# Routing attention and a PReLU FFN on one core: one more pair of heads in cluster order

## The chip, the cores and the metric

The kernel runs on one core of a Trainium2 chip. The metric is device microseconds of one execution. TensorE is PE here (PEld its weight loads), VectorE is DVE, ScalarE is ACT, GpSimd is POOL and SyncE, which issues most transfers, is SP. All engines run their own queue in order.

## The reference

```python
# q, k, v: (4, 8, 768, 64); centroids: (8, 16, 64); w_in: (512, 2048); w_out: (2048, 512)
q_assign = argmax(einsum(q_n, c_n)); k_assign = argmax(einsum(k_n, c_n))   # 16 clusters
mask = q_assign[:, :, :, None] == k_assign[:, :, None, :]
scores = where(mask, q @ k.T / sqrt(64), -1e9)
attn = softmax(scores)
x = (attn @ v).transpose(0, 2, 1, 3).reshape(4 * 768, 512)
h = x @ w_in
out = (maximum(h, 0) + alpha * minimum(h, 0)) @ w_out
```

A query attends only to the keys of its own cluster. The weights come as 64-bit floats and all arithmetic is in 32-bit floats.

## The kernel before, in words

**Pairs and forms.** Two heads make a pair (one in each half of the 128 partitions); pair n is heads 2(n % 4) and 2(n % 4) + 1 of batch n // 4, so there are 16 pairs. Pairs 0 to 8 are dense: for each half of the queries (384) and each of six chunks of 128 keys, PE makes the scores (`score`, L784), ACT the exponential, DVE masks other clusters out (`mask`, L825; in batch 0 PE does that, L793), PE weighs the values (`weigh`, L939), DVE sums the denominators (`add_up`, `turn`, `rows_sums`) and multiplies by the inverse (`normalise`, L1042). Pairs 9 to 15 (`n >= NO`) are ordered: tokens are first sorted by cluster, so that a chunk of keys meets only a window of 224, 320 or 384 of the 768 queries (`window`, `weigh_near` L972, `normalise_near`).

**Ordering a pair.** `load` fetches q and k; `order_features` transposes them (L567); `order_sims` makes the similarities (PE, L575); `order_counts`, `order_begins`, `order_ranks` and `order_rows` turn them into a destination row for each token (DVE, with two tiny products L601). Then `order_stage` loads q, k and v rows into a stage tile (three SP transfers, L661) and `order_scatter` writes each 128 rows to a DRAM scratch by an indirect DMA from POOL (L675): six stages of four scatters. `pace` puts a token from ACT ahead of the scatters of a slot (L651, L652), so that POOL doesn't run ahead. `order_load` reads the sorted pair back (L688 to L706), `order_blocks` transposes it (L713). After the attention the rows go back to token order: `to_rows` (PE transposes L1002), twelve scatters `put_back` (POOL, L1011), `fetch_back` and `turn_back` (L1030).

**Steps and slots.** The program is one hand-written order. `steps` lists the attention steps, three for a half of a dense pair or for a whole ordered pair; a step has five slots (`tick`), and `later` files a piece for a later slot. `load_at` and `prep_at` hold the loads and preparations by step (`ORDERS`: where an ordered pair is loaded; `LEADS`: how many steps before its own start it is read back). FFN pieces of the previous half batch (`ffn_pieces`: `hidden` L1066 with the slope L1058, `final` L1084) are fed evenly between, so that PE always has work. Steps 0 to 23 are batch 0. There, `second_part` has not yet been called: raw buffers, conversion tiles and the members of batch 0 lie in the memory that later holds sorting tiles and five more E tiles.

**Conversion of the weights.** In batch 0, 32 blocks of 128x512 weights come as 64-bit words into one of five raw buffers (`fetch`, L247). `split` (DVE) takes them apart, `scale` (ACT) runs four slots later, `join` (DVE and a product on POOL, L271) two slots after that; the `power` tile between them has three buffers. A raw buffer is free after the join.

**Order of batch 1.** Steps 24 to 47: pairs 4, 5, 6, 7, first halves then second halves, each block of twelve steps with the FFN of one half batch.

Of the kernel before, what the change touches and what calls it, by code (L numbers as in the profile page):

```python
# [23 lines left out]
def kernel(  # L24
# [50 lines left out]
    ps_f = fast.enter_context(tc.tile_pool(name="ps_f", bufs=2, space=PS))  # L75
    fast.enter_context(tc.manual_schedule())
    first_part = fast.enter_context(ExitStack())
    memp = first_part.enter_context(tc.tile_pool(name="memp", bufs=NCH))
    raws = first_part.enter_context(tc.tile_pool(name="raws", bufs=1))
    cvt = first_part.enter_context(tc.tile_pool(name="cvt", bufs=3))  # L80

# [22 lines left out]
    pairs = [(b, hp) for b in range(B) for hp in range(NCH)]  # L104
    NO = WHOLE * NCH - 3
    NP = len(pairs)
# [134 lines left out]

    raw_tiles = [raws.tile([P, CW, 2], U32, name=f"raw{i}") for i in range(5)]

    def convert(src, dst):
        raw = raw_tiles[0]
        raw_tiles.append(raw_tiles.pop(0))
        nc.sync.dma_start(out=raw.rearrange("p n w -> p (n w)"), in_=src)  # L247
        lo, hi = raw[:, :, 0], raw[:, :, 1]
        power = []

        def split():
            power.append(cvt.tile([P, CW], U32, name="power"))
            nc.vector.tensor_scalar(out=power[0], in0=hi, scalar1=0x7FF00000, scalar2=None,
                                    op0=ALU.bitwise_and)
            nc.vector.tensor_scalar(out=dst.bitcast(U32), in0=hi, scalar1=0x000FFFFF,
                                    scalar2=None, op0=ALU.bitwise_and)

        def scale():
            nc.scalar.activation(out=power[0], in_=power[0], func=AF.Relu,
                                 bias=low_exp[:, 0:1], scale=8.0)  # L260
            nc.scalar.activation(out=dst, in_=dst.bitcast(U32), func=AF.Identity,
                                 bias=1.0, scale=2.0 ** -20)

        def join():
            nc.vector.scalar_tensor_tensor(
                out=power[0], in0=hi, scalar=0x80000000, in1=power[0],
                op0=ALU.bitwise_and, op1=ALU.bitwise_or)
            nc.vector.scalar_tensor_tensor(  # L268
                out=dst, in0=lo, scalar=2.0 ** -52, in1=dst,
                op0=ALU.mult, op1=ALU.add)  # L270
            nc.gpsimd.tensor_tensor(out=dst, in0=dst, in1=power[0].bitcast(FP32),  # L271
                                    op=ALU.mult)
        return [split, scale, join]
# [23 lines left out]
    def advance(stages):  # L297
        stages.pop(0)()
        if stages:
            later(4 if len(stages) == 2 else 2, lambda: stages and advance(stages))  # L300
        elif stages is under_way[0]:
            under_way.popleft()
            converted[0] += 1
# [186 lines left out]
    STAGES = 2  # L490
    us, ranks, orders, scratch, sorts = {}, {}, {}, {}, {}
    sorting = deque()

    def second_part():

        first_part.close()
        for name, bufs in (("emore", 1), ("ordc", 1), ("ordp", 1), ("order", NP - NO),
                           ("xmore", 1), ("byrow", 1), ("pace", 8)):
            sorts[name] = fast.enter_context(tc.tile_pool(name=name, bufs=bufs))
        for i in range(5):  # L500
            e_tiles.insert(0, sorts["emore"].tile([P, 2, HS], FP32, name=f"more{i}"))

    def order_constants():

        ordc = sorts["ordc"]
        stage = [ordc.tile([P, NX // PARTS, P], FP32, name=f"stage{i}") for i in range(STAGES)]
        place = ordc.tile([P, HS], U16, name="place")
# [8 lines left out]
        brief = asg.tile([P, HS], FP32, name="simT")  # L516
        assert NX // PARTS > len(kinds)
        own = stage[0][:, 0:len(kinds), :]
        for i, pattern in enumerate(kinds):
# [10 lines left out]
        def columns():  # L530
            nc.vector.tensor_reduce(out=cols, in_=own, axis=AX.X, op=ALU.add)
            for t in stage:
                nc.gpsimd.memset(t, 0.0)

# [24 lines left out]
        for i, piece in enumerate((columns, sums_before, sums_within, shifts)):  # L559
            later(5 + i, piece)  # L560
        begins = ordc.tile([P, NP - NO], FP32, name="begins")
        sorts.update(stage=stage, number=number, place=place, before=before, within=within,
                     shift=shift, begins=begins)
# [41 lines left out]
    def order_ranks(n, ps):  # L605
# [3 lines left out]
        nc.vector.tensor_tensor(out=begin, in0=ps[:, 0:2], in1=sorts["shift"], op=ALU.add)  # L609
        nc.vector.tensor_copy(out=sorts["begins"][:, n - NO:n - NO + 1], in_=ps[:, 0:1])  # L610
        nc.vector.scalar_tensor_tensor(out=count, in0=count, scalar=begin[:, 1:2],
# [3 lines left out]
    def order_rows(n, begin, count):  # L615
# [9 lines left out]
        whole = tc.dram_tile([2 * 2 * S, P], FP32, name=f"scratch{n}")  # L625
        scratch[n] = whole, dram_disjoint_views(whole, 2 * NX)
        for i in range(2 * PARTS + STAGES):
            if i >= STAGES:
                for x in range(NX // PARTS):
                    sorting.append((1, lambda i=i - STAGES, x=x: order_scatter(n, i, x)))  # L630
            if i < 2 * PARTS:
                sorting.append((0, lambda i=i: order_stage(n, i)))
        later(2, lambda: order_clusters(n, begin))
# [20 lines left out]
    def order_stage(n, i):  # L654

        b, hp = pairs[n]
        h, part = divmod(i, PARTS)
# [71 lines left out]
    for b in range(B):  # L729
        whole = [n for n in range(b * NCH, (b + 1) * NCH) if n >= NO]  # L730
        rest = [n for n in range(b * NCH, (b + 1) * NCH) if n < NO]
        begun_at.append(len(steps))
        steps += [(n, None, s) for n in whole for s in range(SB)]
        for half in range(2) if rest else ():
            if half and not whole:
                begun_at.append(len(steps))
            steps += [(n, half, s) for n in rest for s in range(SB)]
            feeds[len(steps)] = [(b, 0), (b, 1)] if whole else [(b, half)]
    begun_at.append(len(steps))
# [137 lines left out]
    def rows_sums(n, half):  # L877
        near = n >= NO
        if not near or half == 0:
# [31 lines left out]
    def spread_out(n, half, inv):  # L911
        pool = sorts["ordp"] if n >= NO and half else rdp
        rd = rds[n, half] = pool.tile([P, HS], FP32, name="rd")
# [120 lines left out]
    def x_tile(b, half):  # L1034
        if (b, half) not in xTs:
            pool = sorts["xmore"] if (b, half) == (WHOLE - 1, 1) else xpool
            xTs[b, half] = pool.tile([P, NCH, HS], FP32, name="xT")
# [104 lines left out]
    def last_pieces():  # L1142
# [197 lines left out]
        def room_for_y():  # L1340
            t = sorts["xmore"].tile([P, NCH, HS], FP32, name="xT").rearrange(
                "p c q -> p (c q)")
# [24 lines left out]

    ORDERS = [26, 29, 35, 38, 41, 56, 60]
    LEADS = [4, 3, 4, 4, 3, 3, 3]
    prep_at, load_at = {}, {}  # L1370
    for (n, half), u in start_of.items():
        def at(step, slot, piece):
            prep_at.setdefault((step, slot), []).append(piece)
        if half is None:
            t = ORDERS[n - NO]
            load_at.setdefault(t, []).append(lambda n=n: load(n))
            for i in range(2):
                at(t + 1, FIRST + i, lambda n=n, i=i: order_features(n, i))
            at(t + 2, 2, lambda n=n: order_sims(n))
            load_at.setdefault(u - LEADS[n - NO], []).append(  # L1380
                lambda n=n: order_load(n))
            at(u - 4, 0, lambda n=n: prep_clusters(n))
            for i in range(2):
                at(u - 1, i, lambda n=n, i=i: order_blocks(n, i))
                at(u - 1, FIRST + i, lambda n=n, i=i: order_queries(n, i))
            continue
        if half == 0:
# [5 lines left out]
            else:  # L1393
                load_at.setdefault(u - (9 if u < 2 * TOGETHER else 10), []).append(
                    lambda n=n: load(n))
# [4 lines left out]
            else:  # L1400
                for w in range(2):
                    at(u - 7, FIRST + w + (u - 7 == TOGETHER - 1),
                       lambda n=n, w=w: prep_blocks(n, w))
            at(u - (3 if n < NCH else 5 if u - 6 < TOGETHER else 6), FIRST,
               lambda n=n: prep_sims(n)) if u - 6 < 2 * TOGETHER else at(
                   u - 6, FIRST + 1, lambda n=n: prep_sims(n))
# [14 lines left out]
    def scatters_at(v, s, i):  # L1421


        if v < SB:
            return 1 + (s == 0 or i == 0)
        if v < 3 * SB:
            return 0
        if v < 4 * SB:
            return int(s == 0 or i == 0)
        return 1 + (s == 0 or i % 2 == 0)  # L1430

# [29 lines left out]
    for u in range(-AHEAD, TOGETHER):  # L1461
        for piece in load_at.get(u, []):
            piece()
        n, half, s = steps[max(u, 0)]
        prior = steps[max(u - 1, 0)]
        ended = u > 0 and prior[2] == SB - 1
# [31 lines left out]
        for i in range(SLOTS - FIRST):  # L1498
# [7 lines left out]
            if u >= -1:  # L1506
                fetch(3 if u < UB else 2)
        if s == SB - 1 and u >= UB:
            total(n)
# [6 lines left out]
    for u in range(TOGETHER, NS + 1):  # L1516
# [50 lines left out]
        else:  # L1567
            slots = range(SLOTS)
        if u == TOGETHER + 1:
            order_constants()  # L1570
        for i in slots:
# [40 lines left out]

    NN, m = NP - NO, 2 * NC
    spans = const.tile([m, 4, NN], FP32, name="spans")
# [203 lines left out]
```

## Time and profile before

| | us |
|---|---|
| median of 14 runs | 932.88 (932.13 to 934.03) |
| the profiled execution | 933.0 |
| its span, first to last instruction | 931.2 |
| PE busy | 916.5 (98%) |
| DVE busy | 656.2 (70%) |
| POOL busy | 385.4 (41%) |
| ACT busy | 262.0 (28%) |
| scatters into the scratch: 168, mean | 1.06 |
| mean DMA rate | 83 GB/s |

The granted TensorE clock is 1.000 over the span. The span is cut into 40 slices of 23.3 us; a digit is the busy share of a slice in tenths. Batch 0 ends at about 196 us, when the scores of pair 4 begin. A group line reads: source line, engine, operation, output and inputs, shapes, number of records, then busy time, mean time of one, and the idle time before them with what ended it.

### The profile page before, as it was taken

Reading aid. Unit: us, or ns where it says so; the run is one execution under the profiler, and the core shown is the slowest. Engines: PE = TensorE matmul, PEld = TensorE weight load, DVE = VectorE, ACT = ScalarE, POOL = GpSimd, SP = SyncE. Lnnn points to the kernel's source line nnn. Section 1 sums busy time; section 2 is a strip of 40 time slices with the busy share of each in tenths; the row PEclk is TensorE's granted clock in tenths of the full one; section 3 lists DMA queues with packets and bytes.
Section 4 is the critical chain, followed back from the end, with each engine's and each line's share of the span. In section 5 each row is a group of like instructions: output and inputs, shape, how many; then the busy total and the mean of one; then the engine's idle time right before and its main releaser. Section 6 shows DMA issues by size and latency. Waiting matters only on the chain.

```text
span 931.2 us, 11983 instructions
## 1 busy us (share of the span) xinstructions
PE 916.5 (98%) x3963; PEld 494.8 (53%) x3963; DVE 656.2 (70%) x1246; ACT 262.0 (28%) x660; POOL 385.4 (41%) x579
## 2 busy tenths in 40 slices
PE   8999999999999999999999999999999999999997
PEld 5434444445445454445555554555555555556886
DVE  5797788889769598598997799764647135598200
ACT  5764444233123122231222332122312120221000
POOL 2332232200006768587766787677733470000000
PEclk9999999999999999999999999999999999999999
DMA  8342648128001525453861383643511012000000
GB/s 301 122 133 93 138 132 160 23 46 188 27 1 48 150 74 150 85 106 82 162 134 37 53 134 100 139 92 89 92 44 26 12 38 54 1 0 1 23 23 26
DMA packets 226708, 77.71 MB, mean 83 GB/s; under 512 B 210752, under 2 KB 214544, under 8 KB 226640
## 3 DMA queue, kind: packets, MB, share of 16 engines
q1 hardware_dynamic: 217728, 62.72, 30.4%
q0 software_dynamic: 8064, 13.78, 4.6%
q8 instruction: 33, 0.54, 0.3%
q10 hardware_dynamic: 848, 0.39, 0.2%
q14 instruction: 35, 0.29, 0.1%
HBM read 52.25 MB, written 24.25 MB: 82 GB/s over the span
## 4 chain that ended last, share of the span: by engine, by line
PE 93%; DVE 4%; issue 1%; ACT 1%; POOL 0%; ACTq 0%; DVEq 0%; POOLq 0%
PE fps L1066 27%; PE fps L1084 27%; PE sps L784 7%; PE vps L939 7%; PE sps L1302 4%; PE sps L1246 4%; PE fps L784 3%; PE vps L1246 2%; PE vps L1302 2%; PE vps L972 1%; PE mps L972 1%; PE fps L1302 1%; PE fps L1246 1%; PE sps L793 1%; PE mps L894 1%
## 5 line engine op out<-in xcount | busy, mean ns | idle before, releaser
L1066 PE MATMUL fps<-xT,w_in_sb 128*128 128x384 f32 x768 | 259.3, 491 | 0.0
L1084 PE MATMUL fps<-w_out_sb,gT 128*128 128x512 f32 x576 | 254.1, 595 | 0.3 <-DVE gT L1058 0.3
L675 POOL DMA_INDIRECT scratch<-stage,off x168 | 177.8, 1059 | 65.5 <-DMA stage<-in_v_dram 28.0
L1066 PEld LDWEIGHTS fps<-xT,w_in_sb 128*128 128x128 f32 x768 | 142.3, 190 | 103.2 <-issue 4.9
L1084 PEld LDWEIGHTS fps<-w_out_sb,gT 128*128 128x128 f32 x576 | 107.5, 190 | 132.2 <-issue 122.6
L652 POOL COPY paced<-pace 1x1 f32<-1x1 f32 x204 | 56.3, 276 | 138.4 <-ACT pace L651 137.8
L1072 ACT COPY gT<-fps 128x384 f32<-128x384 f32 x96 | 45.9, 478 | 236.0 <-PE fps L1066 236.0
L1058 DVE SCALAR_TENSOR_TENSOR gT<-gT,alpha 128x384 f32<-128x384 f32 x96 | 61.5, 648 | 61.1 <-ACT gT L1072 60.9
L1011 POOL DMA_INDIRECT back<-rows,off x84 | 85.8, 1021 | 22.1 <-issue 16.5
L784 PE MATMUL sps<-qkT 64*128 64x384 f32 (+1 forms) x464 | 85.0, 485 | 0.0
L805 ACT ACTIVATE E<-sps 128x768 f32<-128x768 f32 (+1 forms) x76 | 56.4, 786 | 62.1 <-PE sps L793 39.7
L784 PEld LDWEIGHTS sps<-qkT 64*128 64x128 f32 x464 | 41.3, 186 | 38.6 <-issue 15.5
L825 DVE SCALAR_TENSOR_TENSOR more<-aq,key,more 128x384 f32<-128x384 bf16 (+2 forms) x116 | 60.4, 579 | 0.0
L939 PE MATMUL vps<-E,vt 128*64 128x384 f32 x292 | 54.2, 495 | 1.5 <-DVE xT L1042 1.5
L271 POOL TENSOR_TENSOR w_in_sb<-w_in_sb,power 128x512 f32<-128x512 f32 x16 | 24.4, 1523 | 71.1 <-DVE w_in_sb L268 71.1
L271 POOL TENSOR_TENSOR w_out_sb<-w_out_sb,power 128x512 f32<-128x512 f32 x16 | 22.5, 1409 | 55.9 <-DVE w_out_sb L268 55.9
L825 DVE SCALAR_TENSOR_TENSOR E<-aq,key,E 128x384 f32<-128x384 bf16 (+2 forms) x88 | 45.0, 568 | 0.6 <-ACT E L802 0.6
L835 DVE TENSOR_TENSOR acc<-acc,E 128x768 f32<-128x768 f32 x35 | 33.3, 951 | 14.5 <-ACT E L805 13.6
L907 DVE RECIPROCAL inverses<-mps 64x12 f32<-64x12 f32 (+1 forms) x42 | 10.5, 250 | 45.7 <-PE mps L894 45.4
L1090 ACT COPY y<-fps 128x512 f32<-128x512 f32 x18 | 10.5, 586 | 99.2 <-PE fps L1084 99.2
L1092 DVE TENSOR_TENSOR y<-y,fps 128x512 f32<-128x512 f32 x24 | 16.4, 682 | 27.4 <-PE fps L1084 27.4
L805 ACT ACTIVATE more<-sps 128x768 f32<-128x768 f32 (+1 forms) x40 | 29.2, 764 | 12.3 <-PE sps L784 11.8
(284 smaller groups left out, 1177.1 us busy)
## 6 DMA issues: line engine op xcount, KB each, us to landing
raw<-in_moe_w_in_dram SPq DMA_DIRECT2D x16, 512.0 KB, 6.5
raw<-in_moe_w_out_dram SPq DMA_DIRECT2D x16, 512.0 KB, 4.4
out_dram<-y SPq DMA_DIRECT2D x21, 256.0 KB, 2.3
qk<-scratch SPq DMA_DIRECT2D x56, 96.0 KB, 3.2
qk<-in_q_dram SPq DMA_DIRECT2D x48, 96.0 KB, 3.6
qk<-in_k_dram SPq DMA_DIRECT2D x48, 96.0 KB, 3.2
w_in_kept<-w_in_sb SPq DMA_DIRECT2D x8, 512.0 KB, 3.0
vt<-in_v_dram SPq DMA_DIRECT2D x9, 384.0 KB
```

The lines of the kernel that those rows point to most:

```text
L652: nc.gpsimd.tensor_copy(out=sorts["paced"], in_=token)
L675: nc.gpsimd.indirect_dma_start(out=scratch[n][1][h * NX + xx], out_offset=bass.IndirectOffsetOnAxis(ap=ranks[n][:, xx, h:h + 1], axis=0), ...
L784: nc.tensor.matmul(out=bank(ps, h, m), lhsT=qkT[r:r + D, S + c * P:S + (c + 1) * P], rhs=qkT[r:r + D, tokens], start=True, stop=not early_ ...
L805: nc.scalar.activation(out=E[:, :, 0:m], in_=ps[:, :, 0:m], func=AF.Exp, scale=SCALE)
L825: nc.vector.scalar_tensor_tensor(out=e, in0=of, scalar=keys[n][:, NJ + c, h:h + 1], in1=e, op0=ALU.is_equal, op1=ALU.mult)
L939: nc.tensor.matmul(out=po[r:r + D, 0:HS], lhsT=vts[n][:, h, c, :], rhs=e[:, h, :], start=(c == 0), stop=(c == NJ - 1))
L1011: nc.gpsimd.indirect_dma_start(out=to[i], out_offset=bass.IndirectOffsetOnAxis(ap=place[:, h, j:j + 1], axis=0), in_=rows[j // HJ][:, j % ...
L1058: nc.vector.scalar_tensor_tensor(out=gs[f], in0=gs[f], scalar=alpha[:, f:f + 1], in1=gs[f], op0=ALU.mult, op1=ALU.max)
L1066: nc.tensor.matmul(out=ps[:, 0:HS], lhsT=w_in_sb[:, c, f * P:(f + 1) * P], rhs=xTs[b, half][:, c, :], start=(c == 0), stop=(c == NCH - 1))
L1084: nc.tensor.matmul(out=ps[:, 0:DM], lhsT=gs[f][:, i * P:(i + 1) * P], rhs=w_out_sb[:, f, :], start=on and f == f0, stop=off and f == f0 + ...
L1246: nc.tensor.matmul(out=bank[to], lhsT=w_in_form(m, x, cc), rhs=rhs[:, cc, :], start=start and cc == 0, stop=cc == KH - 1, skip_group_check ...
L1302: nc.tensor.matmul(out=bank[to], lhsT=g_form(m, x, t), rhs=w_out_form(n, x), start=start and x == 0, stop=x == NQ - 1, skip_group_check=no ...
```

## The change

Pair 7, the last of batch 1, becomes an ordered pair. It is loaded at step 11 and sorted during steps 12 to 20 of batch 0, read back at step 21, and worked at steps 24 to 26, ahead of pairs 4 to 6. Batch 1 thus has 21 steps instead of 24, with FFN blocks of twelve and nine steps, and all later ordered pairs from pair 11 on are loaded three steps earlier. To make room in batch 0, the sorting tiles are allocated from the start, the `power` tile has two buffers (and one of the y tiles for every third of the first twelve blocks), there are four raw buffers and a fifth that lies in an x tile, for the first eight fetches and the next turn of the ring, scale and join come one slot earlier after the twelfth block, and pair 7's two stages lie in input tiles, cleared when the first is used. Later pairs have two stage tiles of their own. In the sorting queue a stage is issued after two scatters of the next stage in line instead of right after the last scatter that read its tile. The slots of batch 0 take two, two and one scatters. More scatters are allowed per slot before batch 2 and in its last steps. Some x tiles change pools.

```diff
-    cvt = first_part.enter_context(tc.tile_pool(name="cvt", bufs=3))
+    cvt = first_part.enter_context(tc.tile_pool(name="cvt", bufs=2))
...
-    NO = WHOLE * NCH - 3
+    ORDERED = [2 * NCH - 1] + list(range(WHOLE * NCH - 3, B * NCH))
+    NO = ORDERED[1]
...
-    raw_tiles = [raws.tile([P, CW, 2], U32, name=f"raw{i}") for i in range(5)]
+    raw_tiles = [raws.tile([P, CW, 2], U32, name=f"raw{i}") for i in range(4)]
+    first_raw = xpool.tile([P, NCH, HS], FP32, name="xT")...
+    raw_tiles.append(first_raw)
...
-        raw = raw_tiles[0]
-        raw_tiles.append(raw_tiles.pop(0))
+        raw = raw_tiles.pop(0)
+        fetches[0] += 1
+        if raw is not first_raw or fetches[0] < 2 * NCH:
+            raw_tiles.append(raw)
...
-            power.append(cvt.tile([P, CW], U32, name="power"))
+            power.append(ypool.tile([P, DM], FP32, name="y").bitcast(U32)
+                         if i < NCH * 3 and i % 3 == 2 else
+                         cvt.tile([P, CW], U32, name="power"))
...
-            later(4 if len(stages) == 2 else 2, lambda: stages and advance(stages))
+            later((4 if len(stages) == 2 else 2) - (started[0] > NCH * 3),
+                  lambda: stages and advance(stages))
...
         for i in range(2 * PARTS + STAGES):
-            if i >= STAGES:
-                for x in range(NX // PARTS):
-                    sorting.append((1, lambda i=i - STAGES, x=x: order_scatter(n, i, x)))
-            if i < 2 * PARTS:
-                sorting.append((0, lambda i=i: order_stage(n, i)))
+            stage = [(0, lambda i=i: order_stage(n, i))] * (i < 2 * PARTS)
+            scatters = [(1, lambda i=i - STAGES, x=x: order_scatter(n, i, x))
+                        for x in range(NX // PARTS if i >= STAGES else 0)]
+            if i > STAGES:
+                stage_before = held.pop()
+                scatters[2:2] = stage_before
+            if i < STAGES:
+                sorting.extend(stage)
+            else:
+                held.append(stage)
+            sorting.extend(scatters)
...
     def order_stage(n, i):
+        if n == ORDERED[0] and i == 0:
+            stage_tiles([inp.tile([P, 2, NJ, D], FP32, name="qk")... for _ in range(STAGES)])
...
-        whole = [n for n in range(b * NCH, (b + 1) * NCH) if n >= NO]
-        rest = [n for n in range(b * NCH, (b + 1) * NCH) if n < NO]
+        whole = [n for n in range(b * NCH, (b + 1) * NCH) if n in ORDERED]
+        rest = [n for n in range(b * NCH, (b + 1) * NCH) if n not in ORDERED]
...
-            pool = sorts["xmore"] if (b, half) == (WHOLE - 1, 1) else xpool
+            pool = sorts["xmore"] if (b, half) in ((1, 1), (B - 1, 0)) else xpool
...
-    ORDERS = [26, 29, 35, 38, 41, 56, 60]
-    LEADS = [4, 3, 4, 4, 3, 3, 3]
+    ORDERS = [11, 26, 29, 32, 35, 38, 53, 57]
+    LEADS = [3, 4, 3, 4, 4, 3, 3, 3]
...
-            return 1 + (s == 0 or i == 0)
+            return 1 + (s == 0 or i % 3 == 0)
...
-        return 1 + (s == 0 or i % 2 == 0)
+        return 1 + (s == 0 or i != 1)
...
+        if u == ORDERS[0] - 1:
+            order_constants()
...
             if u >= -1:
                 fetch(3 if u < UB else 2)
+            if sorting:
+                pace()
+            room = 1 + (i < 2)
+            while sorting and room:
+                scatters, piece = sorting.popleft()
+                piece()
+                room -= scatters
...
-        if u == TOGETHER + 1:
-            order_constants()
```

## The prediction

> **What bounds the kernel now.** I read the page's engine lines first, then TensorE's (PE's) waits.
>
> ```profile
> PE 916.5 (98%) x3963; PEld 494.8 (53%) x3963; DVE 656.2 (70%) x1246; ACT 262.0 (28%) x660; POOL 385.4 (41%) x579
> ...
> PE   8999999999999999999999999999999999999997
> ...
> DVE  5797788889769598598997799764647135598200
> ...
> POOL 2332232200006768587766787677733470000000
> ```
>
> PE is idle for 14.7 us of the 931.2 us span: 6.4 in the first 100 us, 5.2 after its last matmul, 3.1 between. In slices 4 to 8, where the change puts its new work, VectorE (DVE) is nearly full and GpSimd (POOL) has room.
>
> ```profile
> PE fps L356 <- ACT qkT L360: 1.9, 2, 1.5
> PE vps L939 <- DVE xT L1042: 1.5, 1, 1.5
> PE mps L575 <- issue: 1.4, 1, 1.4
> ...
> PE mps L575 <- ACT rows L1005: 0.9, 1, 0.9
> ...
> PE fps L784 <- ACT E L802: 0.7, 1, 0.7
> ```
>
> Columns: total us, times, longest. No wait of PE is above 2 us, so a matmul taken out is time saved unless a new wait takes its place. [...]
>
> **PE's work.** Pair 7 leaves the dense form (two halves of 384 queries, all six key chunks) for windows of 224, 320 or 384 queries. Groups, busy us and mean ns of a record; one matmul has two records:
>
> ```profile
> L784 PE MATMUL sps<-qkT 64*128 64x384 f32 x408 | 79.0, 500 | 0.0
> L939 PE MATMUL vps<-E,vt 128*64 128x384 f32 x292 | 54.2, 495 | 1.5 <-DVE xT L1042 1.5
> L939 PE MATMUL vps<-more,vt 128*64 128x384 f32 x140 | 24.6, 491 | 0.0
> L784 PE MATMUL fps<-qkT 64*128 64x384 f32 x80 | 17.3, 508 | 0.0
> ...
> L784 PE MATMUL fps<-qkT 64*128 64x320 f32 x56 | 11.4, 457 | 0.7 <-ACT E L802 0.7
> ...
> L784 PE MATMUL sps<-qkT 64*128 64x224 f32 x56 | 8.4, 375 | 0.0
> ...
> L1002 PE MATMUL mps<-ident,qk 128*128 128x128 f32 x42 | 6.9, 273 | 0.0
> ```
>
> Dense pair: 16 score matmuls at 79.0/204 = 0.387 and 8 at 17.3/40 = 0.433 make 9.7 us; 24 of L939 at 78.8/216 = 0.365 make 8.8; denominators (L894) 0.7. Together 19.2. Ordered pair, a seventh of each group: scores 4 x 0.387 + 11.4/7 + 8.4/7 = 4.4; L972 31.1/7 = 4.4; denominators 0.4; transposes back (L1002) 1.0; counts (L601) 0.5. Together 10.7; the cluster matmuls cost the same in both forms. Saved: 8.5 us. The order of time agrees: half a dense pair runs from 322.87 with 2.1 us of scores, 4.0 of L939 and 2.1 of scores, 16.6 per pair against 6.8 for the ordered pair at 463.01 (1.8, 3.3, 1.8); less the extras that is 8.9. I take 8.5.
>
> **DVE in batch 0.** Rows of four stretches, each three steps (12 to 23):
>
> ```profile
> 79.40:110.40 31.00, 30.74 (x117) 13.97 (x115) 21.93 (x37) 12.58 (x21) 7.63 (x5) 1.00 0.33 84
> 110.40:139.90 29.50, 29.50 (x114) 13.87 (x115) 25.55 (x43) 14.71 (x26) 8.57 (x6) 1.00 0.63 146
> 139.90:173.30 33.40, 33.40 (x134) 15.28 (x133) 29.19 (x51) 14.21 (x25) 8.25 (x6) 1.00 0.70 126
> 173.30:202.10 28.80, 28.80 (x133) 13.40 (x132) 23.27 (x38) 8.68 (x16) 3.05 (x4) 1.00 0.15 29
> ```
>
> Columns: length, then PE, PEld, DVE, ACT, POOL busy, granted clock, DMA share. DVE is busy 99.9 of 122.7 us. Added: ordering pair 7 (two transposes L567 at 0.97, seventeen other steps from L404 to L645 at 0.15 to 0.95) 10.3 us; its blocks, queries and keys 4.3; the constants, moved up, 2.6. Leaving for batch 1, because pair 7 now stands ahead of pairs 4 to 6: 6.1 (one argmax of 2.6, keys 0.5, blocks 1.9, queries 1.1). Net +11, half of the free 22.8 us; most falls on steps 12 to 16, the emptiest stretch. Cost on the path: nothing, covered by these 22.8 us and by the four E tiles, which let DVE trail by a step (about 10 us) before scores stop. Without the cover it would be up to 11 us. In batch 1 DVE gets lighter (24 masks at 0.6 and ten sums at 0.95 go).
>
> **POOL in batch 0.** Idle POOL at 115.7 to 167.2 us (steps 16 to 20; starts by the score matmuls) gets 24 scatters, in front of and between ten weight products.
>
> ```profile
> L675 POOL DMA_INDIRECT scratch<-stage,off x168 | 177.8, 1059 | 65.5 <-DMA stage<-in_v_dram 28.0 <-issue 26.3 <-POOL stage L672 7.5
> ...
> L271 POOL TENSOR_TENSOR w_out_sb<-w_out_sb,power 128x512 f32<-128x512 f32 x16 | 22.5, 1409 | 55.9 <-DVE w_out_sb L268 55.9
> ```
>
> Back to back, a scatter with its token takes 1.32 us (282.40 to 283.83, less the number copy's share): 32 us, six number copies 1.6, two clears 1.1, ten products 14: 49 of 51.5 us. So POOL runs full there and trails. Who waits: weight tiles, needed by PE two steps after their product by the order of issue, some 18 us; DVE, since with two power tiles instead of three the next split waits for the product two before it; and the reload of pair 7. Products now stand ahead of their step's scatters, so the split pays only what is left over from the step before. Today it waits 5.3 us in all for POOL in this batch; I allow twice that, inside DVE's room. The scatters use SP too: six stages of three DMAs, 2.4 us to landing, behind the weight fetches. Issued two scatters later, a stage no longer holds SP until the previous scatters land, but has only two scatters' time (2.6 us) of lead; POOL waited 28 us for stages before, and may here for a few.
>
> The reload (L688 to L706 take SP 8.7 us, 3.2 more to land) is issued at step 21 (167.2) and feeds the transposes in step 23 (about 192). Scatters may end at 178 before that is late: 11 us of room. Pair 5's load stands behind it on SP and has less.
>
> A rule against the change: a 2-input DVE operation and a POOL operation that read together. Here two slopes at 126.05 beside a product at 126.22 took 2.17 instead of 1.2 us, but the scatter's mean of 1.06 over 168, most of them beside a busy DVE, is hardly above its usual 0.97. [...] The rows speak against it.
>
> **Conversion and rest.** Raw buffers: five until the tenth fetch, then four; with splits and joins one slot closer I count, by the order of issue, no step where a fetch is missing and no FFN piece that must force a conversion. Fetches come up to a step later, 9 us or more ahead of use, against 4.4 to 6.5 us to landing. Cost 0, bounds 0 to 1. Batch 1 loses three steps; pairs 9 to 15 keep their distance to their scatters' deadline within three steps, and POOL, starting at 275 before, is idle when pair 7's twelve rows go back (16 us). Tiles of x change places without a wait: each was free a block before. Cost 0.
>
> **New waits.** PE meets an order_sims, an order_begins and a reloaded pair in batch 0, where the nearest rows are 1.4, 0.9, 0.7 and 0.3 (L1084 behind a slope). From below: the three later ones (3.1 in all) could go. From above: one of each kind new, 3.3. I take 1.5, the size of the commonest.
>
> **Sum.** Profiled run 933.0 us (span 931.2 and 1.8 around it), the median 932.9: 932.9 - 8.5 + 1.5 = 925.9.
>
> **Rivals.** (1) The reload is late. At 1.94 us a scatter (96 from 275 to 461 in batch 1) POOL needs 47 + 17 us from 118 and ends near 182; the blocks land at 195 and pair 5's load at 202, so scores and the FFN behind DVE wait 3 to 6 us: about 929. For it: stage waits; against: the 11 us of room. (2) Slower: splits trapped behind scatters. If each of ten splits waits for two scatters and a product (4.1 us), DVE loses 41 - 5 = 36; its 8 us of spare in steps 15 to 20 and 10 us of E tiles absorb 18, PE loses 18: 942. It decides the sign when a split waits over some 3.4 us. Against it: the product precedes the scatters of its step. (3) The windows don't hold pair 7 and the fallback runs: excluded, since the inputs' largest reach for it is 71 rows beside a chunk and 96 are allowed (pair 13 needs 90).
>
> **Chances.** 0.2% (1.9 us) is what can be told from no change. Forecast, up to 928.5: 0.68. Rival 1, to 931: 0.12. Between the two slow cases, within 0.2%: 0.06. Rival 2: 0.14. Faster 0.80, same 0.06, slower 0.14. Range 921.5 (8.5 and the 3.1 saved) to 931.5; some 0.19 lies outside.
>
> **What would show it.** Right: L939 falls from 432 records to 384 and L784 from 600 to 576, L972 gains a seventh, PE busy is near 908, idle still 15 to 17. Rival 1: PE idle near the 196 us mark, waiting for DVE L713 or L1042. Rival 2: DVE waiting for POOL L271 by tens of us before L253 and PE for E. Wrong altogether if PE busy does not fall by 7 us or more.

## The result: 11 us slower, with the order of work that was forecast and two waits that were not

The changed kernel takes 944.12 us (median of 6 runs, 943.51 to 946.3) against 932.87 us of the kernel before (28 runs, 931.96 to 934.03): a ratio of 1.0125 [1.0115, 1.0135]. Its profiled execution took 944.78 us, its span is 943.0. Lines behind the diff have moved: scores L784 are now L815, L939 is L970, L972 is L1003, the normalise L1042 is L1073, the FFN's L1066 and L1084 are L1097 and L1115, the slope L1058 is L1089, the split L253 and L255 is L267 and L269, the product L271 is L285, the scatter L675 is L706.

Page of the changed kernel, engines and slices of 23.6 us:

```profile
PE 914.4 (97%) x3931; PEld 494.8 (52%) x3931; DVE 660.5 (70%) x1245; ACT 259.5 (28%) x667; POOL 434.0 (46%) x636
...
PE   8997998999999999999999999999999999999997
...
DVE  5796897979858979678798799864657135598100
...
POOL 2333238820033888758566787687833471000000
PEclk9998998999999999999999999999999999999999
```

PE is busy 2.1 us less, and idle for 943.0 - 914.4 = 28.6 us instead of 14.7. PE's digits fall to 7 and 8 in two places, the fourth slice (71 to 94 us) and the seventh (141 to 165 us), and in the same two the clock row, which was all 9 before, shows an 8. PE's waits say where:

```profile
PE fps L1097 <- DVE xT L1073: 6.4, 1, 6.4
PE fps L1115 <- DVE y L1123: 3.6, 1, 3.6
PE fps L1115 <- DVE gT L1089: 2.1, 3, 1.1
PE fps L815 <- ACT more L833: 1.9, 3, 0.7
PE mps L594 <- ACT rows L1036: 1.6, 2, 0.9
```

Two single waits are 10.0 of the 13.9 us of added idle time. Stretches of the changed kernel (length, then PE, PEld, DVE, ACT, POOL busy, granted clock, DMA share), each wait followed by the work behind it:

```profile
79.85:86.29 6.44, 0.01 (x1) 0.03 (x1) 5.63 (x15) 2.64 (x4) 2.30 (x2) 0.81 0.62 171
86.29:94.48 8.19, 8.19 (x20) 4.46 (x20) 4.94 (x9) 0.96 (x2) 0.00 (x0) 0.73 0.04 13
149.73:153.31 3.58, 0.01 (x2) 0.00 (x1) 2.46 (x4) 0.95 (x2) 3.42 (x4) 0.83 0.41 89
153.31:159.77 6.46, 6.46 (x9) 2.88 (x10) 6.18 (x12) 2.88 (x6) 5.55 (x8) 0.57 1.17 227
```

Behind each wait PE is fully busy, but at a granted clock of 0.73 and 0.57: work of 6.04 us takes 8.19, and work of 3.70 us takes 6.46. The shorter times are those of the same matmuls in e11_s16, one of the repaired kernels below:

```profile
82.33 6.04 PE L1097 MATMUL fps<-xT,w_in_sb 128*128 128x384 f32 x18 [1.84 <-DVE xT L1073]
...
143.84 3.70 PE L1115 MATMUL fps<-w_out_sb,gT 128*128 128x512 f32 x8 [0.47 <-DVE y L1123]
```

The clock of the changed kernel is 0.50 from 83.82 to 90.63 us and from 152.08 to 158.89 us, and 1.00 between:

```profile
83.82:90.63 6.81, 4.34 (x7) 2.52 (x8) 6.54 (x15) 0.56 (x2) 0.83 (x1) 0.50 0.25 84
152.08:158.89 6.81, 5.58 (x7) 2.49 (x8) 6.66 (x14) 3.84 (x7) 5.75 (x9) 0.50 1.06 206
```

PE is busy for 4.34 and 5.58 us at that half clock, which costs half of each, 2.2 and 2.8 us. So 2.15 + 2.76 = 4.9 us of the PE time is the slow clock. The account of the span: +10.0 for the two waits, +4.9 for the clock behind them, +3.9 of other idle time (2.6 of it shorter waits, 1.25 behind the last matmul), and the rest of PE's busy time, -2.1 - 4.9 = -7.0. Together +11.8, the difference of the spans (943.0 - 931.2).

**The first wait.** In the kernel before, the 24 records of this FFN group run without a gap, and the xT that the seventh of them needs is ready in time:

```profile
78.37 8.01 PE L1066 MATMUL fps<-xT,w_in_sb 128*128 128x384 f32 x24
...
79.38 0.56 DVE L1042 TENSOR_TENSOR xT<-vps,rd 128x384 f32<-128x384 f32 x1
```

Timeline of the changed kernel ahead of the wait:

```profile
75.08 0.45 POOL L544 TENSOR_TENSOR y<-row,ident 128x128 f32<-128x128 f32 x1
...
75.57 0.55 DVE L552 TENSOR_REDUCE cols<-y 128x3 f32<-128x384 f32 x1 [3.95 <-POOL y L544]
...
81.26 0.72 ACT L273 ACTIVATE power<-power,low_exp 128x512 uint32<-128x512 uint32 x1 [8.31 <-DVE power L267]
...
83.23 0.37 DVE L976 STREAM_TRANSPOSE simT<-fps 128x192 f32<-128x192 f32 x1
...
85.59 0.56 DVE L1073 TENSOR_TENSOR xT<-vps,rd 128x384 f32<-128x384 f32 x1
...
86.29 0.98 PE L1097 MATMUL fps<-xT,w_in_sb 128*128 128x384 f32 x1 [6.44 <-DVE xT L1073]
```

`order_constants`, moved up with the load of pair 7 to step 10, has GpSimd make three small tables and VectorE sum them (L552). DVE reaches the sum at 71.6 us, while POOL is at a product of the conversion (until 72.75) and has the tables still to make, and stands still for 3.95 us. Then come 3.0 us of its own constants, the joins and splits that were queued behind them, and only then the normalise of pair 3, at 85.59 instead of 79.38 us. ScalarE waits 8.31 us for a split in the same jam. In this step PE has nothing else: the first FFN group has done its matmuls on the three earlier pairs (6 records) and needs this very xT.

**The second wait.** Timeline of the changed kernel:

```profile
136.28 1.26 POOL L522 MEMSET qk<- 128x512 f32 x2
136.82 0.73 SPq L692 DMA_DIRECT2D qk<-in_q_dram  x1
...
141.79 2.10 POOL L706 DMA_INDIRECT scratch<-qk,off  x1 [4.12 <-DVE power L279]
...
149.54 2.48 POOL L285 TENSOR_TENSOR w_out_sb<-w_out_sb,power 128x512 f32<-128x512 f32 x2
...
150.85 1.48 DVE L267 TENSOR_SCALAR power<-raw 128x512 uint32<-128x512 uint32 x1 [3.73 <-POOL w_out_sb L285]
...
152.58 0.67 DVE L1123 TENSOR_TENSOR y<-y,fps 128x512 f32<-128x512 f32 x1
...
153.31 6.46 PE L1115 MATMUL fps<-w_out_sb,gT 128*128 128x512 f32 x8 [3.58 <-DVE y L1123]
```

Pair 7's stage tiles are cleared and loaded only when its first stage is popped from the sorting queue. POOL stands 4 us between the clears and its first scatter at 141.79, while the transfers are under way: the third of them, issued at 138.65, landed at 140.9 (the timeline names a join as the releaser, which ended at 141.4). That the late stage makes the wait is tested in e2_stages below. Five scatters run until 149.5, and two weight products of an earlier step stand behind them. The next split needs their power tile, waits 3.73 us, and behind it in DVE's queue is the addition that would empty PE's result bank.

### The profile page after: what moved, and what is told of

It reads as the page before. It is cut to its first block, busy times and chain, and to the rows that moved or that the text cites. A ratio compares the mean times of both kernels' runs of the same rounds, so it can differ in the third digit from the quotient of the medians.

```text
span 943.0 us, 12075 instructions
## 1 busy us (share of the span) xinstructions
PE 914.4 (97%) x3931; PEld 494.8 (52%) x3931; DVE 660.5 (70%) x1245; ACT 259.5 (28%) x667; POOL 434.0 (46%) x636
## 4 chain that ended last, share of the span: by engine, by line
PE 84%; DVE 10%; issue 2%; POOL 1%; ACT 1%; SPq 0%; DMA 0%; DVEq 0%; POOLq 0%; ACTq 0%
PE fps L1115 25%; PE fps L1097 25%; PE sps L815 6%; PE sps L1333 4%; PE sps L1277 4%; PE vps L970 4%; PE fps L815 2%; PE vps L1277 2%; PE vps L1333 2%; PE vps L1003 1%; PE mps L1003 1%; DVE acc L866 1%; PE fps L1333 1%; PE fps L1277 1%; DVE power L279 1%
## 5 line engine op out<-in xcount | busy, mean ns | idle before, releaser
L1097 PE MATMUL fps<-xT,w_in_sb 128*128 128x384 f32 x768 | 261.0, 493 | 6.4 <-DVE xT L1073 6.4
L1115 PE MATMUL fps<-w_out_sb,gT 128*128 128x512 f32 x576 | 257.9, 601 | 5.7 <-DVE y L1123 3.6
L706 POOL DMA_INDIRECT scratch<-stage,off x168 | 179.9, 1071 | 67.0 <-issue 25.4
L1097 PEld LDWEIGHTS fps<-xT,w_in_sb 128*128 128x128 f32 x768 | 143.5, 191 | 110.6 <-issue 14.3
L1115 PEld LDWEIGHTS fps<-w_out_sb,gT 128*128 128x128 f32 x576 | 108.2, 192 | 139.2 <-issue 126.3
L679 POOL COPY paced<-pace 1x1 f32<-1x1 f32 x217 | 60.3, 278 | 150.2 <-ACT pace L678 144.9
L1042 POOL DMA_INDIRECT back<-rows,off x96 | 99.8, 1040 | 22.7 <-issue 18.8
L1089 DVE SCALAR_TENSOR_TENSOR gT<-gT,alpha 128x384 f32<-128x384 f32 x96 | 57.6, 610 | 65.4 <-ACT gT L1103 65.3
L815 PE MATMUL sps<-qkT 64*128 64x384 f32 (+1 forms) x448 | 82.1, 482 | 0.1
L836 ACT ACTIVATE E<-sps 128x768 f32<-128x768 f32 (+1 forms) x74 | 54.3, 779 | 37.9 <-PE sps L815 22.8
L815 PEld LDWEIGHTS sps<-qkT 64*128 64x128 f32 x448 | 40.2, 186 | 36.2 <-issue 14.2
L856 DVE SCALAR_TENSOR_TENSOR more<-aq,key,more 128x384 f32<-128x384 bf16 (+2 forms) x110 | 56.0, 569 | 0.6 <-ACT more L833 0.6
L970 PE MATMUL vps<-E,vt 128*64 128x384 f32 x284 | 52.6, 496 | 1.4 <-DVE xT L1073 1.4
L856 DVE SCALAR_TENSOR_TENSOR E<-aq,key,E 128x384 f32<-128x384 bf16 (+2 forms) x82 | 41.9, 565 | 0.0
L285 POOL TENSOR_TENSOR w_in_sb<-w_in_sb,power 128x512 f32<-128x512 f32 x13 | 20.5, 1583 | 45.9 <-DVE w_in_sb L282 45.9
L285 POOL TENSOR_TENSOR w_out_sb<-w_out_sb,power 128x512 f32<-128x512 f32 x15 | 20.3, 1356 | 40.2 <-DVE w_out_sb L282 40.1
L678 ACT COPY pace<-ones 1x1 f32<-1x1 f32 x217 | 31.2, 184 | 10.7 <-POOL paced L679 10.7
```

Of the source, the lines that this page charges most:

```text
L679: nc.gpsimd.tensor_copy(out=sorts["paced"], in_=token)
L706: nc.gpsimd.indirect_dma_start(out=scratch[n][1][h * NX + xx], out_offset=bass.IndirectOffsetOnAxis(ap=ranks[n][:, xx, h:h + 1], axis=0), ...
L815: nc.tensor.matmul(out=bank(ps, h, m), lhsT=qkT[r:r + D, S + c * P:S + (c + 1) * P], rhs=qkT[r:r + D, tokens], start=True, stop=not early_ ...
L836: nc.scalar.activation(out=E[:, :, 0:m], in_=ps[:, :, 0:m], func=AF.Exp, scale=SCALE)
L856: nc.vector.scalar_tensor_tensor(out=e, in0=of, scalar=keys[n][:, NJ + c, h:h + 1], in1=e, op0=ALU.is_equal, op1=ALU.mult)
L970: nc.tensor.matmul(out=po[r:r + D, 0:HS], lhsT=vts[n][:, h, c, :], rhs=e[:, h, :], start=(c == 0), stop=(c == NJ - 1))
```

## The experiments

Theory A: the loss is local, made by where two pieces stand (the constants ahead of pair 3's normalise, the late first stage), and by the slow clock behind each wait. B: the conversion with two power tiles and shorter gaps. C: VectorE is simply full there, so a wait that is taken away comes back elsewhere.

The first twelve kernels ran on two other chips, on which the kernel before itself takes 954 us (a0_after, e5 to e7) and 959 us (the others); ratios are to the kernel before on the same chip. To compare stages there, I use the start of one matmul group of batch 1, the first scores behind the FFN block at 295 us: **the mark**. Differences of marks under 1 us say nothing: kernels that are the same up to there already differ by about 1 us at 44 us. It stands at 308.96 us in the changed kernel, and at 306.42 when the changed kernel ran again there (a0_after, ratio 1.0122 [1.008, 1.0164], with waits of 5.5 and 3.6 us).

> The changed kernel as it is, beside the kernel before on the same chip as the next three. Every theory: 1.2% slower than the kernel before, with 6.4 us of idle TensorE ahead of xT in 60 to 100 us and 3.6 us ahead of y in 140 to 160 us. It is the reference for the next three.

### One part at a time

e4_conv is the kernel before with the changed conversion only (raw buffers, power tiles, one slot less).

> The kernel before, with the change's conversion alone: two power tiles and the y tile, four raw buffers and the fifth in an x tile, scale and join one slot earlier after the twelfth block; pair 7 stays dense. Theory A: no wait comes from it without the sort beside it: 932.5 to 934. Theory B: most of the 11 us is here: 939 or more.

Measured: 1.0029 [0.9987, 1.0071]. Neither of the two long waits is there, so B doesn't carry the loss. But at 80 to 100 us PE is busy 17.4 us (19.7 in the kernel before), for two short waits near 80 and 95 us, where the kernel before waits 0.3 us at most:

```profile
PE fps L1096 <- DVE gT L1070: 1.5, 1, 1.5
...
PE fps L1078 <- DVE xT L1054: 1.3, 1, 1.3
```

They are 1.46 and 1.25 us, and from behind them on every matmul of batch 0 comes 2.7 us later against the kernel before than it did ahead of them. So the conversion alone costs 2.7 us.

e1_consts and e2_stages change one place each, e3_both has both:

```diff
-        if u == ORDERS[0] - 1:
+        if u == 7:                       # e1, e3
             order_constants()
...
-                sorting.extend(stage)
+                sorting.extend(stage * (n != ORDERED[0]))          # e2, e3
...
+    for i in range(STAGES):
+        load_at.setdefault(14, []).append(lambda i=i: order_stage(ORDERED[0], i))
```

> The changed kernel, with the constants of the sort made at step 7 instead of step 10. Theory A (two local delays): the 6.4 us in which PE waits for xT at 80 us come from the constants, which stand on DVE and POOL ahead of pair 3's last normalise; moved up they hide in the wait-bound first steps, PE keeps its clock, and the kernel takes 944.1 - 6.4 - some 2.5 of slow clock = about 935. Theory B (the conversion with two power tiles and one slot less between split, scale and join holds DVE up): the wait stays, 942 to 944. Theory C (DVE is simply full in batch 0): the wait turns up a few steps later, 942 to 944.

> The changed kernel, with pair 7's two stage tiles cleared and first loaded at step 14, instead of when the ranks are ready. Theory A: the first five scatters start at once and are off POOL before the next two products; the 3.6 us wait for y at 150 us and the slow clock behind it (some 2.8) go: about 937.5. Theory B: the product still comes late by the number of power tiles, 943 to 944. Theory C: the wait moves to another step, 942 to 944.

> Both edits: constants at step 7 and stages at step 14. Theory A: the gains add, about 928.5, below the kernel before (932.9) by 4. Theory B or C: above 938.

Measured: 1.0164 [1.0119, 1.0209], 1.0185 [1.0138, 1.0233] and 1.0119 [1.0076, 1.0163]. These intervals are too wide to rank them, but the stages speak: each edit removes the wait that it aims at. In e2 PE is busy 18.8 of 20 us at 140 to 160 instead of 15.8, and the mark comes at 304.92. In e1 and e3 the wait of 6.4 us is gone, but at step 7 the constants delay the denominators of an earlier pair. Waits of PE, e3_both:

```profile
PE fps L963 <- DVE simT L976: 3.5, 1, 3.5
```

e3's mark stands at 300.34, 8.6 us ahead of the changed kernel's; A wanted 15. Most of the rest is this new wait of 3.5 us with a slow clock of its own: the clock is 0.50 for 6.83 us behind it.

### A place for the constants

e7_consts0 has them at step -2, where DVE and POOL wait for the first data; e5_fixed adds the early stages.

> One edit: the constants of the ordering are made at step -2. Theory A: the first stall goes with the slow clock behind it, 6.4 + 2.2 = 8.6 us less than the changed kernel (0.991 of it), the second stall stays; no new wait at 65 to 69 us as there was with the constants at step 7. Theory C: a wait of several us takes its place within 60 to 110 us. Theory B: no change.

> Two edits: the constants of the ordering are made at step -2, while VectorE and GpSimd have nothing to do, and pair 7's first two stage tiles are cleared and loaded at step 14. Theory A (two local delays, and the slow clock behind each, cost the time): both stalls go and nothing takes their place, 6.4 + 2.2 + 3.6 + 2.8 = 15 us less than the changed kernel, that is 0.984 of it, and some 0.996 of the kernel before. Theory C (VectorE is full there, the wait only moves): a new wait of TensorE for VectorE of some us between 60 and 110 us, at most 5 us less than the changed kernel. Theory B (the conversion with two power tiles and shorter gaps): no more than the 6 us of the second stall.

Measured: 1.0118 [1.0077, 1.016] and 1.0065 [1.0033, 1.0098]. Again the waits aimed at go (xT 1.2 us in e7, y 0.5 us in e5), and again one comes: POOL can't begin, because the first argmax holds the tile that the tables use, and PE waits 3.2 us for the first masks. e8_c4, at step -4, ahead of that argmax, with the early stages:

> The constants are made at step -4, ahead of the first argmax, which shares a tile with them, and pair 7's first two stage tiles are cleared and loaded at step 14. With the constants at step -2 TensorE waited 3.2 us for the first aq, since the argmax held the tile that GpSimd needed. Theory A: both stalls go, and the start costs 1 to 2 us, since VectorE's 2.6 us of constants stand in its waits for the first transposes: 0.987 of the changed kernel.

Measured: 1.0063 [1.0034, 1.0093]; PE waits 2.9 us for the centroids instead, 1 us more than I allowed. Steps -4, -2 and 7 each cost a wait of about 3 us, and a half clock for 3.41 us (e7) or 6.83 us (e1, e3, e5, e8) behind it: each time DVE's part of the constants stands ahead of something that PE needs soon.

So e9_lazy13 leaves POOL's part at step 10 and moves DVE's part two steps later, behind the normalise; the tables get a result tile to themselves, since they live longer. e10_lazy13 adds the early stages, and e10_lazy21 does this with DVE's part later still (`later(21 + i, piece)`).

```diff
-        brief = asg.tile([P, HS], FP32, name="simT")
-        own = ypool.tile([P, DM], FP32, name="y")[:, 0:len(kinds) * P].rearrange(
+        room = ypool.tile([P, DM], FP32, name="y")
+        own = room[:, 0:len(kinds) * P].rearrange(
...
-            row = (ordc.tile([P, P], FP32, name=f"row{i}") if i else brief[:, 0:P])
+            row = (ordc.tile([P, P], FP32, name=f"row{i}") if i else room[:, 3 * P:4 * P])
...
-        same = brief[:, 2 * P:3 * P]
+        same = room[:, 0:P]
...
-            later(5 + i, piece)
+            later(13 + i, piece)
```

> One edit: the constants stay at step 10, but they use no tile that the argmax or the denominators use, and VectorE's four pieces of them come in step 12, behind pair 3's normalise, so that VectorE no longer waits for GpSimd in step 11. Theory A: the 6.4 us stall and the slow clock behind it go and no other stall takes their place, 7 to 8.6 us less than the changed kernel (0.992); the second stall stays. Theory C (VectorE is full, the wait moves): a new wait of TensorE for VectorE of some us between 85 and 110 us, and 3 us less at most.

> The edit of e9_lazy13, and pair 7's first two stage tiles cleared and loaded at step 14. Theory A: both stalls go, 13 us less than the changed kernel (0.986), and 0.998 of the kernel before on the same chip; a wait of up to 2 us near 104 us (a slope behind the clears on VectorE's path) may stay. Theory C: at best 1.005 of the kernel before.

> As e10_lazy13, with VectorE's pieces of the constants in steps 13 and 14, behind the slopes. Theory A: both stalls go as there, 0.986 of the changed kernel; with less beside the slopes of step 12, the wait near 104 us is at most the 1.1 us that it is in the changed kernel. Theory C: as there.

Measured: 1.0047 [1.0024, 1.007], 1.001 [0.9982, 1.0037] and 1.0017 [0.9996, 1.0039]; marks at 301.91, 298.36 and 300.02. With e9 the wait for xT is 1.36 us and nothing takes its place: for the constants A holds. In e10_lazy21 the wait near 98 us, which was to fall to 1.1 us, is the same 2.07 us as in e10_lazy13, so DVE's part beside the slopes does not make it. e9_lazy5 gives the tables their own tile but leaves every instruction in its place:

> The changed kernel with the constants' scratch in a result tile of their own instead of the tile that the argmax and the denominators use; all instructions keep their order. If VectorE's place behind GpSimd makes the first wait: TensorE still idles 5.5 to 6.4 us ahead of xT near 80 us. If the shared tile makes it: the wait falls to 1.4 us.

```profile
PE fps L1097 <- DVE xT L1073: 6.5, 1, 6.5
```

One run, 946.1 us; the wait is unchanged. The shared tile is not the cause; DVE's place in the queue is.

### Is the slow clock a price of its own?

e6_warm is the changed kernel with 24 matmuls without use ahead of the first FFN piece of step 12:

```diff
             early.clear()
+            ps = misc()
+            for i in range(24):
+                nc.tensor.matmul(out=ps[:, 0:P], lhsT=ident, rhs=ident, start=True, stop=True)
             feed_block(u)
```

> 24 matmuls of 128x128 without use stand ahead of the first piece of the output product in step 12, where TensorE otherwise idles 6.4 us. They make its idle there short, and nothing else comes earlier. If the slow clock behind a long idle is a price of its own (Theory A with the clock): the 18 matmuls behind the wait take about 6.1 us instead of 8.2, the granted clock of 80 to 100 us rises from 0.83 to near 1, and the time falls by 2 us although TensorE has more work. If the clock is only a record without a price: the time stays, or rises by what the dummies overhang.

PE's timeline, e6_warm:

```profile
77.77 5.62 PE L1529 MATMUL mps<-ident 128*128 128x128 f32 x48
83.23 2.10 PE L1097 MATMUL fps<-xT,w_in_sb 128*128 128x384 f32 x6
86.44 6.04 PE L1097 MATMUL fps<-xT,w_in_sb 128*128 128x384 f32 x18 [1.11 <-DVE xT L1073]
```

xT comes no earlier, at 86 us as before, but the 18 records behind it take 6.04 us instead of 8.19 (7.73 in a0_after, on the same chip), and the clock of 80 to 100 us is 1.00 instead of 0.83. PE does 5.6 us more work, and the mark comes 3.2 us earlier than the changed kernel's: 2.15 here, and the rest because the clock is 0.50 for 3.41 us instead of 6.83 behind the second wait. Against a0_after, whose clock does not fall at all behind its second wait, the mark comes 0.65 us earlier, which is no more than the two differ at 44 us. The ratio, 1.0106 [1.006, 1.0151] against 1.0122, is too coarse to show a gain. The stretch itself shows it: the clock behind a long wait is a price of its own, 1.7 to 2.2 us there.

### What is left without the two waits

e10_lazy13 still had a wait of 2.07 us near 98 us, behind which a group of 1.96 us took 2.79. DVE and POOL of e10_lazy13 ahead of it:

```profile
95.01 1.39 POOL L285 TENSOR_TENSOR w_out_sb<-w_out_sb,power 128x512 f32<-128x512 f32 x1 [3.16 <-DVE w_out_sb L282]
95.18 2.42 DVE L269 TENSOR_SCALAR w_in_sb<-raw 128x512 uint32<-128x512 uint32 x1
96.34 0.98 POOL L522 MEMSET qk<- 128x512 f32 x2
```

A step of the split, 0.42 us by itself, takes 2.42 beside POOL's product and clears. e11_s15 and e11_s16 are e10_lazy13 with the stages at steps 15 and 16.

> As e10_lazy13, but the first two stage tiles are cleared and loaded at step 15 instead of 14, so that GpSimd's two clears no longer stand beside the split that is ahead of the slopes of step 13. Theory A: the wait near 98 us falls from 2.07 to 1.15 us and the matmuls behind it keep the full clock, no wait over 1 us near 146 us, 3 us less than e10_lazy13, 0.997 of the kernel before. If the missing 4 us are something else of the change: 1.000 to 1.002 as e10_lazy13.

> The same at step 16. Theory A: as e11_s15, 0.997 of the kernel before, if the stages still land ahead of the first scatter (about 131 us); if not, TensorE again waits for y near 146 us, up to 3.6 us.

Measured, on the chip where the kernel before takes 932.7 us: 933.51 us, 1.0006 [0.9997, 1.0015], and 933.04 us, 1.0003 [0.9994, 1.0012]. The wait near 98 us is 1.15 and 1.14 us, the clock over the span 0.998, and the mark of e11_s16 stands at 297.82, 11.1 us ahead of the changed kernel's, just as its median is 11.1 us lower. So without the two long waits and their clock the whole loss is gone, as A says, but the 0.997 that it promised is not there. Page and PE's waits, e11_s16:

```profile
PE 910.4 (98%) x3931; PEld 493.2 (53%) x3931; DVE 660.6 (71%) x1245; ACT 259.3 (28%) x667; POOL 430.2 (46%) x636
```

```profile
PE fps L815 <- ACT more L833: 1.9, 3, 0.7
PE fps L1097 <- DVE xT L1073: 1.8, 1, 1.8
PE mps L594 <- ACT rows L1036: 1.6, 2, 0.9
PE fps L1115 <- DVE gT L1089: 1.5, 2, 1.1
```

PE is busy 6.1 us less than before and idle 22.1 us instead of 14.7: short waits grew from 9.5 to 15.0 us, and 1.9 more lie behind the last matmul. I asked whether POOL's tables, which make DVE's joins beside them longer, cause the 1.84 us ahead of xT. e12_c12_11 and e12_c12_8 are e11_s16 with the constants at step 12 and DVE's part at `later(11 + i)` and `later(8 + i)`.

> As e11_s16, with the constants made at step 12 instead of 10, and VectorE's pieces of them in step 14, behind the slopes of step 13. If GpSimd's operations beside VectorE's make the waits: the 1.84 us ahead of xT near 82 us falls to 0.5 or less, as the joins at 73 to 78 us are back to 0.68 us, and the time is 1.5 us less than e11_s16, 0.9985 of the kernel before. If VectorE's added work makes them: the wait only moves behind 82 us, and the time stays at 1.000.

> The same with VectorE's pieces half a step earlier, ahead of the slopes of step 13: as e12_c12_11, but the wait for gT near 98 us is longer by up to 0.6 us (the two pieces ahead of the slopes).

Measured: 1.0014 [1.0005, 1.0023] and 1.0016 [1.0007, 1.0025]. POOL runs ahead of the steps and is at the tables by 77 us already. The wait for xT falls to 1.2 us in the first, not to 0.5, and a new one comes 50 us later, which ends when DVE's slope gT (134.97) and POOL's token (135.01) are done:

```profile
135.11 5.39 PE L1115 MATMUL fps<-w_out_sb,gT 128*128 128x512 f32 x12 [1.73 <-POOL paced L679]
```

In e12_c12_8 the wait for gT near 98 us grows from 1.14 to 2.14 us, with 3.41 us of half clock behind it. Here C is right: short waits of batch 0 move when one is taken away. But the 1.2 us at which the wait for xT stops is the 1.25 us of e4_conv: at the places of e11_s16's waits of 1.84 and 1.14 us, the conversion alone makes 1.25 and 1.46. No version beat the kernel before.

**Pair 7's own scores.** Part of what is missing lies outside batch 0. The chunks with windows of 320 queries, in the kernel before (an ordered pair) and for pair 7 in e11_s16:

```profile
464.14 0.70 PE L784 MATMUL fps<-qkT 64*128 64x320 f32 x4
...
203.90 0.70 PE L815 MATMUL fps<-qkT 64*128 64x320 f32 x2
...
205.31 0.80 PE L815 MATMUL fps<-qkT 64*128 64x320 f32 x2 [0.71 <-ACT more L833]
```

In the first line the products of both heads (two records each) run side by side and take 0.70 us together. For pair 7 each head takes that long by itself, and the second waits until ScalarE has read the first's scores (L833); the same happens in the other half of the pair, with a wait of 0.53 us. All scores of pair 7 take 5.26 us of PE time instead of 3.67, and with the waits 2.8 us are lost. It is the same in the changed kernel. That the two heads share one result bank there is an inference; no run gave them two.

Against the forecast e11_s16 misses 7.3 us (0.3 us slower than the kernel before, where 7.0 us less were expected). The conversion's 2.7, these 2.8 and the 1.9 behind the last matmul are of that size; this is an account from the profiles, and no run removed the first two.

## Why the prediction was wrong, step by step

**PE's work: right in kind, 1.5 to 2.4 us too large.** It was to fall by 8.5 us; it fell by 6.1 in e11_s16, where the clock is near full, and by 7.0 in the changed kernel less its slow clock. The groups (the changed kernel, by shape) show which term:

```profile
L815 PE MATMUL sps<-qkT 64*128 64x384 f32 x384 | 75.2, 500 | 0.0
L970 PE MATMUL vps<-E,vt 128*64 128x384 f32 x284 | 52.6, 496 | 1.4 <-DVE xT L1073 1.4
L970 PE MATMUL vps<-more,vt 128*64 128x384 f32 x100 | 17.7, 491 | 0.0
L815 PE MATMUL fps<-qkT 64*128 64x320 f32 x64 | 14.5, 458 | 1.9 <-ACT more L833 1.9
L815 PE MATMUL fps<-qkT 64*128 64x384 f32 x64 | 13.8, 508 | 0.0
L815 PE MATMUL sps<-qkT 64*128 64x224 f32 x64 | 10.1, 375 | 0.1
```

L970 went from 432 records to 384 and from 78.8 to 70.3 us, 8.5 against 8.8 forecast. The four groups of scores went from 116.1 to 113.6 us: 2.5 saved where the sum had 9.7 - 4.4 = 5.3. The means of the seven other ordered pairs didn't hold for pair 7: its windows of 320 queries took 3.1 us and not 11.4/7 = 1.6, for the reason shown above. The term for L972 erred the other way: the 31.1 us add up groups that overlap in time, L972 keeps PE busy for 23.5 us in all, and the new pair added 3.4 us and not 4.4. So the total of 8.5 was nearer than its terms, by luck: without this slip it would have been 9.5.

**VectorE in batch 0, cost 0: the step that failed.** The +11 us were set against 22.8 us of free time in a stretch of 123 us, but 2.6 of them, the constants, stand in one place of an in-order queue, behind a product of the conversion on POOL and ahead of the one normalise that the first FFN group waits for. The sum priced their duration and not their wait for POOL (3.95 us), nor who stood behind it. The four E tiles that were to let DVE trail by a step cover scores; they don't cover xT. This step cost 6.44 + 2.15 us; with DVE's part moved behind the normalise 1.4 to 1.8 us of wait were left, of which the conversion alone makes 1.25.

**New waits, 1.5 us (bounds -3.1 to +3.3): mis-sized.** They measure 13.9 us in all in the changed kernel and 7.4 in e11_s16, without the two long ones; 1.2 and 1.9 of these lie behind the last matmul. And idle time was priced at its face value. That 3.6 us of it can make the next 3.7 us of work last 6.5 had no term.

**Conversion, cost 0 (bounds 0 to 1): mis-sized.** It measures 2.7 us by itself, in e4_conv.

**POOL and the splits.** The load on POOL was about right (busy 46.0 of the 60 us from 140 to 200, where the sum had 49 of 51.5), and the splits' waits for POOL are 5.6 us in all, where the kernel before has 6.5 (the 5.3 of the prediction leave out 1.2 us at a product of the output weights); I had allowed twice the 5.3. But what counted was one wait of 3.73 us with y's addition behind it, at 3.58 + 2.76 us of PE time. That is rival 2's mechanism, over its own threshold of 3.4 us, once and not ten times; the rival's 942 us is near the result for a reason that is only half its own. The stage's "two scatters of lead" was weighed for later stages; the first stage, which has none, was not.

**What held.** Rival 1 did not come: PE is busy all of 160 to 200 us, and the reloaded blocks were in time. The scatters of batch 0 average 1.15 us beside a busy DVE, near the 1.06 of the kernel before. The sign "wrong altogether if PE busy does not fall by 7 us" fired at -2.1, and a part of it was the clock and not the work.

## What to carry to other kernels

Free time of an engine over a stage doesn't cover an instruction that waits on another engine: ask where it stands in its queue, what is still queued on the engine it waits for, and which instruction behind it feeds the bound engine. Issue the producer early and the consumer late, behind the next result that the bound engine needs. Price an idle stretch of TensorE of some microseconds with the slow work behind it as well, nearly double for the second wait here.

## What the runs showed of the hardware

**The clock behind a wait.** In batch 0, waits of PE up to 1.89 us kept the clock at 1.00 in the profiles read here, and waits of 1.90 to 3.57 us went either way. Where the clock fell, it was 0.50 for 3.41 or 6.83 us: behind 1.90 us in e7_consts0 and 2.07 us in e10_lazy13, but not behind 2.06 us in e2_stages. Behind 6.44 us the work ran 1.36 times as long, behind 3.58 us 1.75 times, behind 2.07 us (e10_lazy13) 1.4 times; but in a0_after the work behind 3.57 us took its full-speed 3.70. The Trainium skill's "TensorE: Matmul & The Clock Gate", section "Part 1: The HAM clock gate", says that the array falls to half clock after an idle window of about 3.4 us, and that the window runs freely, so that the same kernel can meet it differently. The runs agree in the rate, 0.50, and in the chance; the waits of 1.90 and 2.07 us are shorter than that window.

**GpSimd beside VectorE.** The split's single-input step is 0.42 us by itself, 1.50 in several places beside a product, and 2.42 beside a product and two clears. The prediction looked for this in the scatters, where it is not to be seen; it was in the products and the clears, with waits of PE near 98 us behind it.

What stays open: the 1.2 to 1.9 us more behind the last matmul (the instructions there are the same), and why the two heads of pair 7 wait for each other's scores while those of most other ordered pairs don't.
